# Loading the first half's v in rows of three tokens and ordering it on TensorE with 0/1 matrices, with a new written-out order

## The chip, the cores and the metric

The kernel runs on one core of one Trainium2 chip. A core has TensorE for matrix products (PE in the profile; PEld is its loading of the stationary operand), VectorE (DVE), ScalarE (ACT), GpSimd (POOL) and a queue engine (SP) that issues most of the transfers. Transfers between the main memory and the core's on-chip memory run on 16 DMA engines. TensorE writes only to eight PSUM banks of 128 x 512 float32; the other engines empty them.

The metric is the device time of one execution in microseconds (us), lower is better.

## The reference

Masked attention for 4 batches, 8 heads, 768 tokens and head size 64, and behind it a two-branch feed-forward layer on the joined heads. Three of the heads see all earlier tokens; the other five see the first 4 tokens and a window of 64.

```python
scores = scale * np.matmul(q, k.transpose(0, 1, 3, 2))
...
scores = np.where(mask[None, :, :, :], scores, -1000000000.0)
scores = scores - np.max(scores, axis=-1, keepdims=True)
a = np.exp(scores)
a = a / (np.sum(a, axis=-1, keepdims=True) + 1e-09)
return np.matmul(a, v).astype(np.float32)
...
h1 = x @ w1
h2 = x @ w2
g = np.maximum(h1, h2)
return (g @ w_out).astype(np.float32)
```

Here x has 3072 rows (batch times token) of 512, w1 and w2 are 512 x 1024, w_out is 1024 x 512. All inputs and the output are float32; the kernel computes in bfloat16 with float32 sums.

## The kernel before

The work is cut into eight halves, (batch, half) with 384 tokens each, in the order (0,0), (1,0), (0,1), (1,1), (2,0), (2,1), (3,0), (3,1). A half has three blocks of 128 tokens, and its eight heads are taken as four pairs. The heads are sorted at run time, so that the three full ones come first; the casts read the head number from a register.

For one half the steps are: load q, k and v (`load_half`, L416); cast q and k to bfloat16 into `qb` (`cast_qk`, L632) and v into `vb` (`cast_v`, L646); turn q and k so that the head's 64 values lie on the partitions, for early halves on TensorE (`turn`, L664, and `unturn`, the copy out of PSUM), for the halves in `TURNED_BY_DMA` by a DMA on SP (L687); scores on TensorE (L878, for half (0,0) with the mask added by matmuls at L847); exponentials on ACT (L897); masks on DVE (L916); weighted sums with v on TensorE (L941); division on DVE (L958 and L968) into `x`; turning x on TensorE (L1065) into `xt` or by a DMA (L1084).

The feed-forward layer is rewritten: max(h1, h2) = h2 + relu(x (w1 - w2)). So DVE subtracts the weights once (L1101, four pieces), TensorE multiplies w2 with w_out once (turning w2 at L1118, products at L1145, copied out as `w2o`), and each half then does `up` (L1168: eight groups of four products of 384 columns, relu on ACT or DVE at L1191 and L1193) and `down` (L1223: for each of three blocks twelve products of 512 columns).

The float32 loads go to three slots of one buffer `ld`. Half (0,0) has slot 0, w2 slot 1, w_out slot 0 again piece by piece after the casts of (0,0) have read it, w1 slot 2, half (1,0) slot 0 after the casts of w_out, half (0,1) slot 1 after w2 is used. q and k of early halves come as one transfer each (`whole`, L424): partition p gets the tokens 3p, 3p+1 and 3p+2 of each head, a run of 768 bytes. The tokens are put in order when the turned copy leaves PSUM. v comes in three transfers of 128 tokens (`piece`, L437), a run of 256 bytes for each token and head, since v's tokens must lie on the partitions in order.

The order on every engine is written out. `PLAN` (L172) lists the operations by number, in the order in which they were made, with the engine's letter (p PE, a ACT, v DVE, g POOL, s SP) and for TensorE the PSUM banks; each engine works through its own tokens in that order. A token x stands for a short matmul with no use (L359), which keeps TensorE at work while it waits. Constants such as `DMA_TURN` and the numbers given to `op(...)` are the planner's costs: they made the list, and do nothing on the chip. Numbers 0 and 1 load q and k of half (0,0), 2, 3 and 4 its v; 5 and 10 load the halves of w2; 6, 8, 11 and 13 the quarters of w_out; 15 and 18 the halves of w1; 16, 17 and 19 to 21 are q, k and v of half (1,0); 22 to 26 those of half (0,1). SP issues them in the order 1, 0, 2, 4, 3, 5, 6, 8, 10, 11, 13, 15, 18, 16, 17, 21, 19, 23, 20, 22.

Of the kernel before, what the change touches and what calls it, by code (L numbers as in the profile page):

```python
# [13 lines left out]
ALU = mybir.AluOpType  # L14
# [158 lines left out]
1s x0*3 0s x0*5 2s x0*40 4s 44a 42v 52g x0*2 54a 32v x0 49p0 34a 30g x1*2 50a 59p1 62v x2 39p2 64a x3*2 40a x3  # L173
28v 69p3 60a 29v x4*2 70a x4 27v x4*4 3s 31g 63v x4*2 51a x4*3 33g x4*2 41a x4*5 43a x4*3 61g x4*3 37p4 53g
47p5 5s 67p6 38v x7 57p7 6s x0*3 68v x0 58a x0 71p02 48v 8s x1*2 74p13 73a 72a 10s 35v 65g 56v 77p47 36a 11s
55g 76a 45v 80p65 75a 66v 46v 79a 83p20 13s 81a 90p3 82a 86p17 85a 15s 114v 84a 118v 89p6 87a 115p5 7g 88a
119p0 116v 78a 99p2 100p1 120v 105p 95p 18s 9g 91p 131p7 106v 96v 92v 108v 129p5 94v 130p4 107v 132p 93v 144p0
97v 145p 98v 122v 101p 133p 126v 134p 123p1 102v 16s 12g 103v 127p6 104v 128a 124v x3 111p3 109p2 14g 112v
135p 110v 137p 136p 142p 138p 143v 140p 139a 17s 113v 146p 141a 147p 148a 117v 201p1 203p6 202a 207p3 21s 121v
205p2 208a 204v 212p7 206a 125v 214p5 213a 19s 175g 187a 211p4 159g 151v 161g 215v 218p0 173v 149v 165p1 189v  # L180
179p3 219a 155p6 209p2 180a 156v 23s 188g 166a 160v 150a 193p7 162v 210p5 174a 190v 152a 20s 176v 194v 167p0
157p3 195p6 168a 181p1 158v 216p7 196a 22s 171v 182a 169v 232p03 199v 197v 236p61 183v 234a 185v 217v 238a
x3*2 237a 239p31 233a 244p76 222p 26s 240a 235v 246a 242v 229p 241a 247v 24s 178v 153g 191a 163v 245a 220p
230a 177v 192v 186a 154v 248p03 200a 243v 252p61 198v 250a 256p74 221p 164v 25s 253a 290v 170v 254a 285v 226p
291v 258a 172v 418s 255v 249a 265p3 266p 284a 184v 260p6 261p 267v 257a 251v 294p1 417s 227a 288p4 262v 223p
295a 259v 228s 263v 301g 415s 289a 269v 286g 270p0 268v 272p 300g 271p7 273v 224a 276p 264v 351p51 312g 355p34
277v 293g 275v 353a 358p62 292g 419s 279v 287g 352a 304p1 278v 299g 274v 357a 361p75 311g 354v 280p0 356a 313g
363a 282p4 310v 388p3 281a 303g 389p 283v 231s 314p5 317g 297v 360a 330p4 663s 302v 359a 296v 309g 332p0 298v
307a 319a 322p2 331v 305a 315v 326p6 362a 664s 420g 328p4 426a 442v 421g 316v 443a 324p1 435a 434g 416s 323v
446p7 333a 329v 427g 334p5 225s 325a 306v 447a 318v 430p2 327v 320p0 431a 308v 794s 335v 390p 391p 448v 321a  # L190
432v 364p41 392v 369p76 799s 393v 365a 372p52 394v 346p0 370a 367v 373a 542s 429v 444g 422v 445a 347p 366a
423v 449a 428v 348p 437v 374a 433v 436v 371a 544s 375v 376p43 441g 368v 380p75 378a 384p12 341p6 377a 349v
545s 386a 379v 342p 385a 382a 343p 387v 381a 401p3 667s 383v 344a 403p 395p4 396p 404v 397p 405v 402p0 407p
406v 424p2 408v 398v 336p1 409v 425a 399v 668s 573g 564v 337p 547a 553g 574a 410v 548a 338p 400v 563g 546s
554a 411p5 339v 481p76 543s 485p32 412v 483a 488p04 413p1 486a 438p5 795s 414v 551p6 487a 439v 452p3 489a
460p1 482a 552v 665s 490a 462p2 453v 461a 454p0 440v 463v 666s 549a 550g 491p57 575g 576v 455a 494p64 340s
556g 499p13 493a 566v 502p20 565g 495a 670s 456p7 555v 500a 497v 464p6 496a 484v 671s 503a 450p1 457v 501a
498v 518p4 504a 465v 519p 525p2 492a 451v 798s 672g 526p 673a 520p 505v 506p73 678a 686v 345s 510p06 679v 508a
514p51 687v 527p 507a 521p 466p3 562v 528v 923s 522v 512a 529v 530v 511a 471p7 524v 515a 683s 513v 557p6 516a
509v 567p2 560a 532p0 796s 695a 517v 458p5 568a 523v 350s 577p1 537p 459a 531p4 571v 569v 582g 533p 578a 476p2  # L200
538v 534v 690s 539v 570a 535v 477p 536v 677s 558a 540v 581v 478p 579v 694a 572v 559v 580a 561v 541s 467p 684v
479a 468p 699s 614p51 469v 618p40 621p62 616a 472p 924s 615a 470s 623a 473p 617v 622a 625v 620a 642p3 624v
626p15 619a 474v 630p26 628a 634p04 643p 627a 629v 638p57 635a 644v 647p1 645v 797s 631a 648p 593p0 646v 640a
649v 802s 700v 632a 595p2 650v 651v 594a 585p3 633v 596a 676s 639a 591p7 586v 636a 589p6 641v 637v 597p1 590a
592v 927s 809g 803a 652p0 810v 804g 609p2 475s 598v 587p5 669s 654p 583p3 682s 820a 588v 819a 655v 599p4 656v
584v 691s 653p6 657v 658p 600p 659v 660v 661v 480s 601p 610p 602a 662s 675g 688g 697a 611p 681g 674a 830v 689a
696a 733p71 680a 698s 692v 829a 612v 737p53 740p06 926s 734a 604p4 701v 738a 741a 605p 693a 739a 606p 742a
743p27 735a 607v 746p50 751p36 745a 736v 748a 754p14 808s 716p7 753a 750v 823s 708p0 755a 744a 704p6 752a 709v
814s 710p1 685a 705v 756a 603s 747a 770p2 757v 813s 771p 711a 772p 749v 773p 717a 706p3 774v 775v 758p04 776v
707a 762p65 800s 766p17 760a 712p2 763a 833s 817v 815v 777p3 764a 713v 714p4 759a 765v 778p 767a 779p 761v  # L210
702p6 768a 807s 780v 784p5 715a 782v 783p2 703a 769v 723p0 834s 781v 789p 785p 724p 790v 801s 786v 792v 787v
718p1 824s 788v 791v 719p 870p74 793s 837v 874p63 877p25 835v 871a 720p 875a 876a 872a 725p 921s 812v 832g
721a 873v 728p7 822g 879a 922s 825v 805a 878a 831g 729p 827v 811a 838g 881v 806a 882p63 836a 886p41 890p52
818v 730p 821v 888a 816v 828g 826v 891a 898p1 919s 892a 841p5 880v 883a 726v 884a 843p2 842a 893v 920s 887a
839p6 885v 844a 889v 853p3 840a 925s 845p0 722s 854a 908p5 608s 846a 894p42 903p6 727s 896a 847p3 895a 613s
897v 851p0 848v 928a 929g 855p2 943v 934a 942g 933s 852v 935a 849p4 950a 951v 932s 944g 931v 930a 910p 937a
904p 899p 936v 952a 909p3 911v 850a 945v 914p 865p0 913v 731a 915v 953v 941a 938s 866p 949v 957a 905v 916v
907v 867p 917v 906v 939s 856p 900v 912v 868a 901v 946s 989p47 902v 993p36 947s 991a 996p50 857p 994a 995a
860p1 858v 998a 918s 997a 940v 861p 990a 999p73 992v 1002p60 955s 1000a 1007p25 1004a 1026p4 954s 948v 1027p
1009a 1006v 1028p 732s 862p 1003a 1008a 1005v 1010p70 1001a 1014p56 1033p2 1012a 1029p 1011a 1013v 1034p 1030v  # L220
863a 1035p 859s 1031v 970p3 1016a 1036v 1032v 864s 962p0 1015a 1038v 869s 1037v 968p7 956v 1017v 1018p16 969a
# [22 lines left out]
NQK = 8  # L244
# [1406 lines left out]
```

## Time and profile before

| What | us |
|---|---|
| median of three runs | 182.32 |
| lowest and highest of them | 181.66, 182.47 |
| the profiled execution | 182.37 |
| its span in the profile | 180.6 |
| PE busy in the span | 168.2 |
| ACT busy | 121.4 |
| DVE busy | 118.2 |
| POOL busy | 30.7 |

The profile shows one execution, in microseconds from the start of its span. A group's row has the line of the code, the engine, the operation, what it writes and reads, the shapes, the count, the busy time and the mean duration in ns, and then the idle time of the engine just before these instructions with what ended it. A row of a view by stages has the stage, its length, and for PE, PEld, DVE, ACT and POOL the busy time with the number of instructions; then the granted clock, the share of the DMA engines and the GB/s moved. A row of the timeline has the start, the length, the engine, the operation and the count. A matmul's length includes the time until its result stands in PSUM, so the next one starts before it ends.

### The profile page before, as it was taken

How to read it: one execution, taken by the hardware profiler on the slowest of the kernel's cores; microseconds unless marked ns; L12 is line 12 of the kernel's file. 1: busy time of each engine (PE TensorE's matmuls, PEld its weight loads, DVE VectorE, ACT ScalarE, POOL GpSimd, SP SyncE). 2: the span in 40 equal slices, each digit the busy share in tenths (PEclk: the TensorE clock that was granted, in tenths of full speed). 3: DMA queues.
4: the chain of work that ended last, by engine and by line, in shares of the span. 5: the costliest groups of instructions: out<-in, count | busy, mean ns of one | idle time of the engine just before them, and what ended most of it. 6: DMA issues, size and time to landing. Idle time of an engine off the chain costs nothing.

```text
span 180.6 us, 4847 instructions
## 1 busy us (share of the span) xinstructions
PE 168.2 (93%) x1758; PEld 103.2 (57%) x1778; DVE 118.2 (65%) x339; ACT 121.4 (67%) x267; POOL 30.7 (17%) x74
## 2 busy tenths in 40 slices
PE   7998999989999999999999999999999999999950
PEld 7955564554766566676465445755564566455430
DVE  5336979878998987899497444795567477214220
ACT  3659136699999978899796199929995987212110
POOL 6522240302744103220002020021020000000000
PEclk9999999999999999999999999999999999999995
DMA  4999999999999899998479994449954461331040
GB/s 126 304 302 387 387 385 334 204 318 225 291 314 218 180 331 208 220 256 221 104 191 229 127 239 126 107 100 209 247 184 88 107 222 61 87 119 55 4 174 16
DMA packets 78736, 36.17 MB, mean 200 GB/s; under 512 B 62194, under 2 KB 72690, under 8 KB 78706
## 3 DMA queue, kind: packets, MB, share of 16 engines
q1 hardware_dynamic: 78560, 35.73, 75.9%
q8 instruction: 16, 0.26, 0.7%
q14 instruction: 14, 0.11, 0.3%
q10 hardware_dynamic: 146, 0.07, 0.1%
HBM read 25.17 MB, written 6.29 MB: 174 GB/s over the span
## 4 chain that ended last, share of the span: by engine, by line
PE 58%; DMA 20%; DVE 7%; ACT 5%; issue 3%; POOL 2%; SPq 1%; DVEq 1%; POOLq 0%; ACTq 0%
PE ps L1223 25%; PE ps L1168 19%; DMA ld<-in_q_dram 11%; PE ps L878 6%; PE ps L941 5%; DMA ld<-in_moe_w_out_dram 5%; ACT at L897 4%; DMA qk<-qb 3%; PE ps L664 2%; DVE qb L371 1%; DVE at L916 1%; DVE x L968 1%; SPq L442 1%; PE ps L1065 1%; POOL qb L371 1%
## 5 line engine op out<-in xcount | busy, mean ns | idle before, releaser
L897 ACT ACTIVATE at<-ps 128x512 bf16<-128x512 f32 (+2 forms) x134 | 63.6, 576 | 7.8 <-PE ps L878 7.7
L1168 PE MATMUL ps<-xt,w 128*128 128x384 bf16 x256 | 45.9, 326 | 0.3 <-DVE w L1101 0.2
L1223 PE MATMUL ps<-wob,g 128*128 128x512 bf16 (+2 forms) x195 | 44.7, 370 | 0.5 <-issue 0.3
L916 DVE TENSOR_TENSOR at<-at,tab 128x1024 bf16<-128x1024 bf16 (+5 forms) x49 | 24.0, 508 | 15.0 <-ACT at L897 14.8
L1168 PEld LDWEIGHTS <-w 128*128 128x128 bf16 x256 | 23.8, 98 | 15.9 <-DVE w L1101 0.9
L1223 PEld LDWEIGHTS <-g 128*128 128x128 bf16 x200 | 18.5, 98 | 20.4 <-issue 0.2
L1191 ACT ACTIVATE g<-ps 128x384 bf16<-128x384 f32 x34 | 16.5, 501 | 12.2 <-PE ps L1168 12.1
L1223 PE MATMUL ps<-w2o,xt 128*128 128x512 bf16 (+2 forms) x88 | 23.4, 370 | 0.7 <-issue 0.2
L968 DVE TENSOR_TENSOR x<-ps,rez 128x192 f32 x64 | 22.8, 357 | 1.8
L941 PEld LDWEIGHTS <-at 128*128 128x128 bf16 x477 | 18.1, 97 | 5.5 <-ACT at L897 0.8
L1193 DVE TENSOR_SCALAR g<-ps 128x384 bf16<-128x384 f32 x30 | 16.3, 552 | 7.3 <-PE ps L1168 7.0
L878 PE MATMUL ps<-qk 64*128 64x128 bf16 (+1 forms) x330 | 19.9, 228 | 1.1 <-ACT at L897 0.6
L941 PE MATMUL ps<-vb,at 128*128 128x65 bf16 x387 | 19.9, 193 | 0.4 <-ACT at L897 0.2
L878 PEld LDWEIGHTS <-qk 64*128 64x128 bf16 x330 | 12.5, 94 | 10.7 <-issue 8.6
L371 POOL CAST qb<-ld 128x384 bf16 (+1 forms) x24 | 10.9, 478 | 45.1 <-PE ps L1168 17.8
L369 ACT COPY ot<-ps 128x512 f32<-128x512 f32 (+2 forms) x14 | 7.9, 566 | 14.9 <-PE ps L1223 14.8
L371 DVE COPY ot<-ps 128x512 f32<-128x512 f32 x11 | 7.5, 686 | 13.7 <-PE ps L1223 13.7
L371 POOL CAST vb<-ld 128x192 bf16 x22 | 7.9, 390 | 39.9 <-DMA ld<-in_v_dram 29.2
L369 ACT CAST qb<-ld 128x384 bf16 (+1 forms) x31 | 12.7, 466 | 3.0 <-DMA ld<-in_k_dram 1.9
L1223 PEld LDWEIGHTS <-xt 128*128 128x128 bf16 x100 | 9.0, 98 | 8.7 <-issue 0.2
L369 ACT COPY qk<-ps 128x384 bf16<-128x384 bf16 (+1 forms) x19 | 11.3, 639 | 2.5 <-PE ps L664 2.5
L371 DVE CAST qb<-ld 128x384 bf16 (+1 forms) x25 | 8.4, 369 | 6.1 <-DMA qk<-qb 2.5
(67 smaller groups left out, 156.5 us busy)
## 6 DMA issues: line engine op xcount, KB each, us to landing
ld<-in_v_dram SPq DMA_DIRECT2D x24, 256.0 KB, 6.4
out_dram<-ot SPq DMA_DIRECT2D x23, 256.0 KB, 3.3
ld<-in_moe_w_dram SPq DMA_DIRECT2D x4, 1024.0 KB, 10.6
ld<-in_k_dram SPq DMA_DIRECT2D x5, 768.0 KB, 7.1
ld<-in_q_dram SPq DMA_DIRECT2D x5, 768.0 KB, 7.6
ld<-in_q_dram SPq DMA_DIRECT2D x9, 256.0 KB, 4.8
ld<-in_k_dram SPq DMA_DIRECT2D x9, 256.0 KB, 4.5
ld<-in_moe_w_out_dram SPq DMA_DIRECT2D x4, 512.0 KB, 9.2
```

Source lines behind the costliest of these rows:

```text
L369: nc.scalar.copy(out=out, in_=in_)
L371: eng[e].tensor_copy(out=out, in_=in_)
L664: nc.tensor.transpose(to[:, i], qbs[:, T["qb", n, hf] % NQB, t, i].rearrange("p h d -> p (h d)"), ident)
L878: nc.tensor.matmul(to.rearrange("p (i c) -> p i c", c=128), lhsT=lhsT, rhs=q_of(n, i, m)[rows], start=bk not in under, stop=True, skip_gro ...
L897: nc.scalar.activation(out=at[:, bk, 0:w], in_=bank(("ps", b, hf, t), part=bk)[:, 0:w], func=ACT.Exp, scale=scale,)
L916: eng[e].tensor_tensor(out=at, in0=at, in1=tbl, op=ALU.mult)
L941: nc.tensor.matmul(po[:, hh, i - NT * hf, :], lhsT=ats[:, T["at", b, hf, t] % NAT, bk, e * 128:(e + 1) * 128], rhs=rhs, start=first, stop= ...
L968: nc.vector.tensor_tensor(out=xs[:, HALVES.index((b, hf)) % NX, :, bass.ds(heads[2 * p + hh], 1), :], in0=po[:, hh, :, 0:D].unsqueeze(2), ...
L1168: nc.tensor.matmul(bank(key)[:, 0:HALF], lhsT=w[:, kc, fc * 128:(fc + 1) * 128], rhs=xts[:, HALVES.index((b, hf)) % NXT, :, kc, :], start= ...
L1191: nc.scalar.activation(out=g, in_=ph, func=ACT.Relu)
L1193: nc.vector.tensor_scalar_max(out=g, in0=ph, scalar1=0.0)
L1223: nc.tensor.matmul(bank(key)[:, cols], lhsT=lhsT, rhs=(w2o if kind == "x" else wob)[:, c, cols], start=(e == 0), stop=(e == len(steps) - 1),)
```

## The change

v of half (0,0) comes as q and k do: one transfer with three tokens in a row on each partition (`whole` is called for all three). Eight casts (`cast_rows`) put it into bfloat16 in a third of the `xt` buffer that no half uses yet. Then for each block of 128 tokens three products (`spread_v`) with 0/1 matrices put the tokens in order in a PSUM bank, and one copy (`take_v`) on DVE or ACT brings them to `vb`. The 0/1 matrices are three shifted views of one table of 388 columns, which one memset and one POOL instruction write into a part of the second `g` buffer. The weighted sums of half (0,0) wait for the copies out of PSUM. The first half that writes this `xt` and `g` waits for the products.

Three costs of the planner change, with no instruction of their own: a turn by DMA counts 1.2 instead of 0.55 on SP, and the transfer times of turns are smaller. The whole order is new. In it the numbers from 5 on are smaller by two up to the mask tables; 29 is the table of the 0/1 matrices, 34 to 41 are the casts, 42, 44 and 46 the products, 43, 45 and 47 the copies.

```diff
 PLAN = """
-1s x0*3 0s x0*5 2s x0*40 4s 44a 42v 52g x0*2 54a 32v x0 49p0 34a 30g x1*2 50a 59p1 62v x2 39p2 64a x3*2 40a x3
...
-55g 76a 45v 80p65 75a 66v 46v 79a 83p20 13s 81a 90p3 82a 86p17 85a 15s 114v 84a 118v 89p6 87a 115p5 7g 88a
...
+0s x0*3 1s x0*5 2s x0*40 8s 52a 54v 62g x0*3 32a x0 56p0 60a 25g x1*2 30a 57v x1 68g 64p1 70a x2 48p2 29g 65v
+x3 72p3 49a 73v x4*2 28g x4*6 3s 31a x4 53g x4*4 33a x4 69g x4*3 4s 71a x4*2 55g x4 50p4 63a x5 74p5 61g 51a
+58p6 26g x7*2 66p7 75a 59v x0 76p01 67a 27g 79p23 9s 36a 37v 40g 78a 35v 6s 38a 82p45 34v 81a 39v 85p67 41v
+80a 83a 46p1 86a 16s 127v 44p3 87a 11s 131v 84a 128p2 45a 47v 42p4 77a 129v 132p6 43a 88p75 133v 13s 119v
+91p31 90a 123v 89a 120p0 5v 93a 124p2 92a 121v 105p4 95p6 125a 10g 110p 149p5 111v 136p7 113v 112v 135p1 7a
...
 """
...
-DMA_TURN = 0.25
+DMA_TURN = 0.14
+DMA_TURN_X = 0.165
+TURN_ISSUE = 1.2
+V_ISSUE = 0.8
+SPREAD = ((0, 0),)
...
+    spread = gs[:, NG - 1].rearrange("p c f -> p (c f)")[:, 0:388]
...
+    if SPREAD:
+        nc.vector.memset(spread, 0.0)
...
-            if t < 2 and long:
-                whole(t, (q, k)[t])
+            if t < 2 and long or (b, hf) in SPREAD:
+                whole(t, (q, k, v)[t])
...
+            src = lds[:, slot_of[b, hf], 2, bass.ds(heads[2 * p + hh], 1), :]
+            dst = xts[:, NXT - 1].rearrange("p i k c -> p (i k c)").rearrange("p (j h d) -> p j h d", j=NT, d=D)
+            copy(e, dst[:, :, 2 * p + hh, :], src.rearrange("p o (n d) -> p (o n) d", d=D))
...
+            for j in range(NT):
+                at = 128 * i - j + 2
+                nc.tensor.matmul(
+                    bank(("pv", b, hf, i)), lhsT=spread[:, at:at + 128], rhs=src[:, j], start=(j == 0), stop=(j == NT - 1),
+                )
...
+            copy(
+                e, vbs[:, n:n + HP, :, NT * hf + i, 0:D],
+                bank(("pv", b, hf, i)).rearrange("p (n h d) -> p n h d", h=2, d=D),
+            )
...
+        nc.gpsimd.affine_select(
+            out=spread, in_=spread, pattern=[[1, 388]], compare_op=ALU.not_equal, fill=1.0, base=-2,
+            channel_multiplier=-3,
+        )
...
+            o = pe("TX", mm(*[512] * NT), spread_v(b, hf, i), [*cs, *spread_in], claims=[(key, 1)])
...
-                        {"SP": 0.55}, turn_by_dma(n, hf, t), [*cs, *old_s], data=DMA_TURN * NT,
+                        {"SP": TURN_ISSUE}, turn_by_dma(n, hf, t), [*cs, *old_s], data=DMA_TURN * NT,
```

More of the change, by code (lines that the diff above doesn't have):

```diff
@@ L178 @@
[L178 to L182, printed above, removed]
@@ new lines, in tile_three_full_heads, with spread_half @@
+    if SPREAD:
+        spread_in.append(op({"POOL": 0.9}, spread_table, bias_in, rank=RANK["table"], tag="table", port=("POOL",)))
+    def spread_half(b, hf):
+        got = []
+        old = [o for at in spread_ops.values() for o in at]
+        cs = []
+        for p in range(HP):
+            for hh in range(2):
+                cs.append(op(
+                    dict(CAST_V), cast_rows(b * HP + p, hf, hh), [*loads[b, hf, 2], registers, *old],
+                    tag=f"vcast{b}.{hf}.{p}", rank=rank_of("vcast", b, hf, p), port=("POOL", "DVE"), bias=BIAS if b else None,
+                ))
+        leaves((b, hf), (2,), cs)
+        olds = [o for n in range(b * HP, b * HP + HP) for o in last_w.get(n - NQK, ())]
+        spread_ops[b, hf] = []
+        for i in range(NT):
+            key = ("pv", b, hf, i)
+            o = pe("TX", mm(*[512] * NT), spread_v(b, hf, i), [*cs, *spread_in], claims=[(key, 1)])
+            spread_ops[b, hf].append(o)
+            got.append(op(
+                {"DVE": 0.6, "ACT": act(512)}, take_v(b, hf, i), [o, *olds], frees=[key], tag=f"vtake{b}.{hf}",
+                rank=rank_of("vcast", b, hf),
+            ))
+        return got
```

133 lines of the change are left out of this document (80 added, 53 removed).

## The prediction

> **What bounds the kernel now.** I read the page first, then the stages, then the chain of waits.
>
> ```profile
> span 180.6 us, 4847 instructions
> PE 168.2 (93%) x1758; PEld 103.2 (57%) x1778; DVE 118.2 (65%) x339; ACT 121.4 (67%) x267; POOL 30.7 (17%) x74
> ```
>
> ```profile
> 10.43:28.14 17.71, 16.39 (x187) 9.27 (x187) 12.74 (x31) 8.97 (x18) 4.80 (x6) 1.00 1.06 376
> 28.14:50.10 21.96, 20.35 (x214) 12.53 (x217) 18.98 (x56) 17.97 (x42) 6.04 (x16) 1.00 1.05 272
> 50.10:100.00 49.90, 49.55 (x578) 31.62 (x584) 41.40 (x116) 43.62 (x92) 9.65 (x21) 1.00 0.92 224
> 100.00:120.00 20.00, 19.20 (x214) 11.19 (x215) 11.70 (x32) 14.84 (x34) 1.05 (x3) 1.00 0.79 148
> 120.00:174.00 54.00, 53.35 (x461) 29.78 (x466) 28.10 (x78) 30.65 (x69) 3.00 (x8) 1.00 0.46 124
> ```
>
> ```profile
> 10.26 8.38 DMA ld<-in_moe_w_out_dram
> ...
> 19.77 11.38 DMA ld<-in_q_dram
> 31.14 1.13 DVE w L1101
> ...
> 35.10 8.36 DMA ld<-in_q_dram
> 43.59 0.12 DVE qb L371
> ...
> 50.10 0.63 PE ps L1065 x8
> ```
>
> The stages begin where the first scores start (10.43). PE idles 17.71 - 16.39 = 1.32 us until the first `up` (28.14), 21.96 - 20.35 = 1.61 until 50.1, then 0.35, 0.80 and 0.65. The chain runs through loads and their casts until 50.1 and mostly along PE behind it. So up to 50.1 two limits lie close together: the stream of loads, and PE's own work with 2.9 us of idle time in it. Whoever makes the loads earlier and PE's work longer gains only what the two leave.
>
> **The loads.** v of half (0,0) moves 128 x 8 x 3 runs of 256 bytes, 0.786 MB; after the change 1024 runs of 768, as q and k have.
>
> ```profile
> 5.00:8.00 3.00, 2.85 (x37) 2.57 (x36) 1.30 (x6) 1.96 (x7) 1.37 (x4) 1.00 1.13 320
> 8.00:11.00 3.00, 3.00 (x52) 2.52 (x51) 1.73 (x4) 2.01 (x7) 1.22 (x4) 1.00 1.33 227
> 12.00:27.00 15.00, 14.02 (x167) 8.27 (x162) 10.88 (x28) 6.95 (x14) 4.80 (x6) 1.00 1.05 386
> ```
>
> ```profile
> 1.31 0.56 SPq L429 DMA_DIRECT2D ld<-in_q_dram  x1
> 1.92 6.29 SPq L442 DMA_DIRECT2D ld<-in_v_dram  x3
> 8.25 1.06 SPq L531 DMA_DIRECT2D ld<-in_moe_w_dram  x1
> ...
> 8.54 1.22 POOL L371 CAST qb<-ld 128x192 bf16 x4 [1.63 <-DMA ld<-in_q_dram]
> ...
> 13.32 1.39 DVE L371 CAST vb<-ld 128x192 bf16 x5 [2.17 <-DMA ld<-in_v_dram]
> ```
>
> From 5 to 8 us the stream is mostly q and k (320 GB/s), from 8 to 11 mostly v (227), from 12 on weights (386). 0.786 MB take 3.46 us at 227 and 2.46 at 320: **1.0 us** saved, and w2, w_out, w1 and q, k of (1,0) come that much earlier, since the DMA engines are full (share over 1) and drain SP's transfers roughly in order. The bounds: 0 if the stream doesn't care, and 2.4, if v lands 2.4 us behind the second of q and k (8.5, the POOL row) instead of 4.8 (13.3, the DVE row). SP's three v issues (6.29 us) shrink to one of 0.56, so w2 is issued near 2.5 instead of 8.25; that is worth nothing by itself, as the queue ahead of it is still full then. SP's next wait is w_out, which needs casts of q in slot 0 (around 9) as before; it stands behind both halves of w2 now, whose 2.1 MB cover it.
>
> **The added work.** Nine products of 512 columns, three copies, a memset, a table.
>
> ```profile
> 85.16 3.62 PE L1223 MATMUL ps<-wob,g 128*128 128x512 bf16 x16
> ...
> L371 DVE CAST vb<-ld 128x192 bf16 x11 | 3.1, 345 | 2.2 <-DMA ld<-in_v_dram 2.2
> ...
> L369 ACT CAST w2o<-ps 128x512 bf16<-128x512 f32 x3 | 1.7, 588 | 2.4 <-PE ps L1145 2.4
> L371 DVE CAST w2o<-ps 128x512 bf16<-128x512 f32 x1 | 0.7, 693 | 1.0 <-PE ps L1145 1.0
> L1536 POOL TENSOR_SCALAR_AFFINE_SELECT tab<-tab 128x384 bf16<-128x384 bf16 x2 | 1.0, 520 | 0.1
> L1585 DVE MEMSET tab<- 128x576 uint32 x1 | 0.5, 538 | 1.0 <-PEq L1632 1.0
> ```
>
> - **PE:** sixteen products of this shape take 3.62 us in a row, 0.226 each: nine take **2.0 us**, none of it in waits for the weights' loading.
> - **Casts:** eight before (5 DVE, 2 POOL, 1 ACT), eight after (5, 1, 2), 0.345 each: nothing.
> - **Copies:** two on ACT at 0.588, one on DVE at 0.693. ACT has them among the exponentials of (0,0), where the plan has PE do other work; ACT is busy 8.97 of 17.71 us there, DVE 12.74. Cost nothing while the weighted sums stand behind the turning of w2, as the new list has them; without that cover 1.2 us, two copies in a row on ACT.
> - **Table and memset:** 0.52 us on POOL, and at most 0.54 on DVE (the table has fewer columns than the row's), both before 8 us, where these engines wait for q and k. The mask tables go from DVE to POOL as well; I take nothing, and at worst the scores start by one POOL cast, 0.35 us, later.
>
> Half (0,0)'s `xt` and `g` guests are gone long before the third and second half write there: nothing.
>
> **Where the 2.0 us land.**
>
> ```profile
> 13.52 0.60 PE L847 MATMUL ps<-tab 128*128 128x512 bf16 x2
> ...
> 14.69 0.42 PE L941 MATMUL ps<-vb,at 128*128 128x65 bf16 x8 [0.24 <-ACT at L897]
> ...
> 16.71 1.22 PE L1118 MATMUL ps<-tab,w2b 128*128 128x128 bf16 x16 [0.48 <-DVE w2b L371]
> ...
> 28.14 0.34 PE L1168 MATMUL ps<-xt,w 128*128 128x384 bf16 x1 [0.19 <-DVE w L1101]
> ```
>
> ```profile
> 0.00:10.43 10.43, 8.41 (x88) 7.67 (x88) 0.20 (x1) 1.00 0.89 216
> 10.43:28.14 17.71, 0.67 (x6) 0.21 (x3) 0.00 (x0) 1.00 1.06 376
> 28.14:40.00 11.86, 0.27 (x2) 0.19 (x2) 0.00 (x0) 1.00 1.07 277
> ```
>
> The second view is the useless matmuls alone. There are 88 before the first scores, time that the products can't use, since v has not landed. The new list puts them behind the fourth group of scores, which by the first row here ends near 13.5. From 10.43 to 28.14 PE can give them the 1.32 us of idle time and some 0.2 of three useless matmuls (three weight loads in their row, whose 0.67 counts what hangs over from before 10.43): waits for w2 (0.48), exponentials (0.24) and the subtraction (0.19) are of that kind, and the earlier loads help with the first and last. So PE is 2.0 - 1.5 = **0.5 us** behind at the first `up`'s place at best, with the full 2.0 as the other bound.
>
> From 28 to 50 there are 1.61 us of idle time more, and 0.1 of useless matmuls:
>
> ```profile
> PE ps L359 <- ACT at L897: 0.6, 1, 0.6
> PE ps L1223 <- issue: 0.5, 3, 0.2
> PE ps L941 <- DVE vx L371: 0.4, 1, 0.4
> PE ps L878 <- DVE x L968: 0.3, 1, 0.3
> ```
>
> These are among PE's longest waits from 28 to 174. The one for `vx` hangs on v of (1,0), which follows the weights in the queue; the one at L359 (0.6) lies between the scores of (1,0), where the new list has six useless matmuls instead of two, so a wait stays there. If all went, PE would reach 50.1's place 1.7 - 0.5 = 1.2 us earlier; the loads allow 1.0, and more only with the landing bound. I leave 0.6 us of waits in place: 0.5 + 0.6 - 1.7 = **-0.6 us**.
>
> **The rest of the order** moves the same work. What it can win is the 0.80 + 0.65 us of idle time behind 100; what it can lose has no floor in the profile. The planner's dearer turn is close to the chip:
>
> ```profile
> L687 SPq DMA_TRANSPOSE qk<-qb x24: 1178/1250/2544, 81.4 to 144.7; - x24
> ```
>
> 1.25 us on SP where 0.55 was planned, so the old list was made with a cost less than half of the true one. I take 0, from -1.1 to +0.8.
>
> **The sum:** loads only as a limit, PE +2.0, idle time -2.6 (1.5 + 1.7 - 0.6), order 0: -0.6. The profiled execution took 182.37 us for its span of 180.6, and lies 0.05 from the median of 182.32. 182.37 - 0.6 = **181.8 us**, by itself from 181.2 (no idle time left) to 182.6.
>
> **The rivals.**
>
> - *The later waits go too.* With turns planned at their price the stage from 100 to 120 loses its 0.80, and the last some of its 0.65: 1.1 us more, **180.7**. For it: the turn's row. Against it: 0.5 of the named waits are "issue", which no order takes away.
> - *PE has room that its busy share hides,* so that the products cost nothing. The weight loading is busy for 57% of the span only. Then the loads are the limit, -1.0 or a little more: **181.3**. Against it: sixteen products in 3.62 us leave no gap between them. The Trainium skill, Perfetto Trace Analysis, Identifying the Most-Contended Engine, says that a share of busy matmul time is a bad measure of how near TensorE is to its limit, and that the share of LDWEIGHTS is a better one; by that rule PE at 57% has room. The row at 85.16 doesn't agree for this shape.
> - *The products wait for v (slower).* They stand in PE's fixed order between the fourth and fifth group of scores, so the turning of w2, the last scores and all weighted sums queue behind them. PE gets there near 13.5; the casts take 1.4 (five in a row on DVE). So it decides at a landing of 12.1: earlier costs nothing, later costs one for one. 8.5 + 2.4 gives 10.9; but if v lands at 13.3 as now, PE stands 1.2 us, the stage's idle time is spent there, 0.3 is left to take the products: +2.0 + 1.2 - 1.5 = 1.7, and 0.2 comes back later. **183.9**.
> - *It doesn't do what it says:* the whole v moves no faster. Then PE's 0.5 stays and nothing comes back: **182.9**. Against it: 320 against 227 GB/s.
>
> **How the numbers follow.** About 0.5% (0.9 us: 181.4 and 183.2) is what a measurement of this kernel can tell from no change. Forecast 0.40 (0.08 of it below 181.4, 0.32 within), later waits too 0.22 (faster), room in PE 0.06 (faster), products wait 0.22 (slower), v no faster 0.10 (0.08 within, 0.02 slower, with new waits). Faster 0.36, same 0.40, slower 0.24. The range of 180.5 to 183.9 leaves out half of the waiting case and under half of the best one, 0.2 in all; the forecast's own is 181.2 to 182.6.
>
> **What would show it.** Right: casts of v start near 11 instead of 13.3, GB/s from 8 to 11 near 320, nine products in 2.0 us with less than 0.3 of waiting before them, the first `up` between 26.5 and 29, w1's last subtraction starting before 30.5, and PE busy 2 us more less some useless matmuls. Wrong: an idle PE ahead of the products, scores of (0,0) that start behind 10.8, or an idle time of PE behind 50 that differs from 1.8 by more than 0.5; then the new order, not v, made the time.

## The result and the profile after

| | median us | runs | ratio to before | 95% interval |
|---|---|---|---|---|
| before, first comparison | 182.32 | 5 | | |
| after, first comparison | 180.75 | 5 | 0.9918 | 0.9889 to 0.9947 |
| before, later comparison | 181.63 | 23 | | |
| after, later comparison | 181.38 | 12 | 0.9982 | 0.9951 to 1.0014 |

The first comparison is the one that the prediction was made for: 180.75 us, 0.8% faster, inside the range of 180.5 to 183.9 and 1.05 below the forecast of 181.8. The second, made for the experiments, found 0.2% with an interval that includes no change. In the two profiled executions of after PE's work ends at 172.81 and 172.78 us; in three of before's order (one written with the new source) it ends at 174.13, 173.86 and 173.57, so 0.8 to 1.3 us later. The gain is small, between nothing and 1%.

The profile after, from its page:

```profile
span 179.1 us, 4862 instructions
PE 168.3 (94%) x1759; PEld 103.0 (57%) x1781; DVE 116.9 (65%) x326; ACT 124.5 (70%) x279; POOL 31.5 (18%) x80
```

PE is as busy as before (168.2), although it does nine more products (the two busy sums are taken up again near the end); the span is 1.5 us shorter. The same stages as in the prediction, each from the first scores, the first `up` and so on (columns: stage, its length, then busy time and instructions of PE, PEld, DVE, ACT and POOL, granted clock, DMA share, GB/s):

```profile
9.93:26.56 16.63, 15.46 (x182) 9.08 (x183) 13.21 (x30) 10.81 (x21) 2.87 (x4) 1.00 1.05 384
26.56:48.87 22.31, 21.79 (x218) 13.31 (x219) 19.05 (x53) 17.91 (x44) 4.51 (x12) 1.00 1.07 270
48.87:100.00 51.13, 50.37 (x591) 31.54 (x595) 39.16 (x107) 46.92 (x105) 12.42 (x30) 1.00 0.95 219
100.00:120.00 20.00, 19.61 (x221) 11.53 (x225) 12.65 (x39) 16.19 (x36) 2.26 (x6) 1.00 0.58 137
120.00:172.70 52.70, 52.38 (x457) 29.45 (x459) 27.72 (x74) 27.39 (x60) 1.66 (x4) 1.00 0.50 132
```

Length less busy time is PE's idle time: 1.17, 0.52, 0.76, 0.39 and 0.32 us, 3.16 in all, where before had 1.32, 1.61, 0.35, 0.80 and 0.65, 4.73 in all. The largest drop, 1.1 us, is in the second stage. Some 1.2 to 1.5 us of each total are no waits: the traces lack 20 (before) and 22 (after) records of matmuls, all of 512 columns, and nearly each leaves a gap of about 0.05 or 0.16 us. The stages don't hold the same work in both orders either. And the first scores start 0.50 us earlier (9.93 instead of 10.43), ahead of all these stages. The loads, in the same view of after and then in its timelines of POOL and DVE:

```profile
5.00:8.00 3.00, 2.85 (x43) 2.52 (x42) 1.90 (x6) 1.84 (x6) 2.58 (x7) 1.00 1.10 331
8.00:11.00 3.00, 2.88 (x43) 1.99 (x40) 1.18 (x4) 2.64 (x9) 2.77 (x7) 1.00 1.08 347
```

```profile
8.29 1.22 POOL L378 CAST qb<-ld 128x192 bf16 x4 [0.23 <-DMA ld<-in_k_dram]
...
10.65 1.39 DVE L378 CAST xt<-ld 128x192 bf16 x5 [0.30 <-DMA ld<-in_v_dram]
```

From 8 to 11 us the stream moves 347 GB/s instead of 227, and the casts of v start at 10.65 instead of 13.32. PE's timeline of after around the products:

```profile
12.57 0.40 PE L953 MATMUL ps<-qk 64*128 64x128 bf16 x8
12.90 1.47 PE L717 MATMUL ps<-xt,g 128*128 128x512 bf16 x6
14.21 0.61 PE L1195 MATMUL ps<-tab,w2b 128*128 128x128 bf16 x8
14.66 0.81 PE L717 MATMUL ps<-xt,g 128*128 128x512 bf16 x3
15.30 0.61 PE L1195 MATMUL ps<-tab,w2b 128*128 128x128 bf16 x8
...
18.04 1.22 PE L1195 MATMUL ps<-tab,w2b 128*128 128x128 bf16 x16 [0.49 <-DVE w2b L378]
...
22.44 2.32 PE L1222 MATMUL ps<-wob,w2t 128*128 128x512 bf16 x10
...
26.56 0.81 PE L1245 MATMUL ps<-xt,w 128*128 128x384 bf16 x4
```

No wait stands ahead of the products (a row that had one would show it in brackets). They take the turnings of w2 between them, and the next turnings still wait 0.49 us for w2. The first `up` comes 1.58 us earlier than in before, but that is not the lead of PE: the new order puts ten of the 32 products of w2 and w_out behind it (22 of their weight loads stand ahead of it instead of 32). At 0.216 us each (the row at 22.44 has ten in 2.32 us, the last of them 0.379 long) they are 2.2 us, so with equal work done PE would be at 28.7, 0.6 us behind before.

### The profile page after: what moved, and what is told of

The parts are those of the page before. It is cut to its first block, busy times and chain, and to the rows that moved or that the text cites. A ratio compares the mean times of both kernels' runs of the same rounds, so it can differ in the third digit from the quotient of the medians.

```text
span 179.1 us, 4862 instructions
## 1 busy us (share of the span) xinstructions
PE 168.3 (94%) x1759; PEld 103.0 (57%) x1781; DVE 116.9 (65%) x326; ACT 124.5 (70%) x279; POOL 31.5 (18%) x80
## 4 chain that ended last, share of the span: by engine, by line
PE 59%; DMA 17%; ACT 8%; DVE 5%; issue 4%; POOL 2%; SPq 1%; DVEq 0%; ACTq 0%; POOLq 0%
PE ps L1302 26%; PE ps L1245 18%; DMA ld<-in_moe_w_out_dram 6%; PE ps L953 6%; PE ps L1016 6%; ACT at L972 5%; DMA ld<-in_q_dram 5%; DMA ld<-in_v_dram 4%; PE ps L674 2%; DVE at L991 2%; DMA qk<-qb 1%; ACT qb L376 1%; POOL qb L378 1%; DMA raw<-in_is_retrieval_dram 1%; ACT vx L376 1%
## 5 line engine op out<-in xcount | busy, mean ns | idle before, releaser
L1245 PE MATMUL ps<-xt,w 128*128 128x384 bf16 x256 | 45.2, 326 | 0.0
L991 DVE TENSOR_TENSOR at<-at,tab 128x1024 bf16<-128x1024 bf16 (+5 forms) x49 | 24.3, 509 | 12.9 <-ACT at L972 12.1
L1270 ACT ACTIVATE g<-ps 128x384 bf16<-128x384 f32 x33 | 15.9, 505 | 12.0 <-PE ps L1245 11.9
L378 POOL CAST qb<-ld 128x384 bf16 (+1 forms) x28 | 11.8, 454 | 54.8 <-PE ps L1245 19.6
L376 ACT COPY ot<-ps 128x512 f32<-128x512 f32 (+1 forms) x16 | 9.1, 575 | 16.4 <-PE ps L1302 15.4
L953 PE MATMUL ps<-qk 64*128 64x128 bf16 (+1 forms) x330 | 19.1, 228 | 0.2
L953 PEld LDWEIGHTS <-qk 64*128 64x128 bf16 x330 | 12.1, 94 | 9.3 <-issue 7.0
L376 ACT CAST qb<-ld 128x384 bf16 (+1 forms) x35 | 13.7, 453 | 3.9 <-DMA ld<-in_q_dram 2.5
L378 DVE COPY qk<-ps 128x384 bf16<-128x384 bf16 (+1 forms) x14 | 9.6, 697 | 4.2 <-PE ps L674 4.0
L378 POOL CAST vb<-ld 128x192 bf16 x18 | 5.8, 357 | 32.3 <-DMA ld<-in_v_dram 29.1
L378 DVE COPY ot<-ps 128x512 f32<-128x512 f32 (+1 forms) x9 | 6.1, 674 | 8.0 <-PE ps L1302 8.0
L1033 DVE RECIPROCAL rez<-ps 128x6 f32<-128x6 f32 x32 | 5.7, 187 | 6.3 <-ACT at L972 4.0
## 6 DMA issues: line engine op xcount, KB each, us to landing
ld<-in_moe_w_dram SPq DMA_DIRECT2D x4, 1024.0 KB, 12.1
```

The source lines that it names most:

```text
L376: nc.scalar.copy(out=out, in_=in_)
L378: eng[e].tensor_copy(out=out, in_=in_)
L953: nc.tensor.matmul(to.rearrange("p (i c) -> p i c", c=128), lhsT=lhsT, rhs=q_of(n, i, m)[rows], start=bk not in under, stop=True, skip_gro ...
L991: eng[e].tensor_tensor(out=at, in0=at, in1=tbl, op=ALU.mult)
L1033: nc.vector.reciprocal(out=z, in_=po[:, :, :, D])
L1245: nc.tensor.matmul(bank(key)[:, 0:HALF], lhsT=w[:, kc, fc * 128:(fc + 1) * 128], rhs=xts[:, HALVES.index((b, hf)) % NXT, :, kc, :], start= ...
```

## The experiments

Each ratio is against runs of before on the same chip.

### The change taken apart: order, load and products

Four kernels cross the order, the load and the products. `WHOLE_V` is a constant that loads v of half (0,0) in one transfer without the products; the two kernels that have this leave v's tokens out of order, so they show times only. In the new order without products, the eight casts stand where the row casts stood. Here and below only the part of `PLAN` that matters is shown, without regard to its line breaks.

New order, v in pieces, no products:

```diff
-SPREAD = ((0, 0),)
+SPREAD = ()
+WHOLE_V = ()
 PLAN = """
-0s x0*3 1s x0*5 2s x0*40 8s 52a
+0s x0*3 1s x0*5 2s 4s 3s x0*40 10s 41a
...
-83a 46p1 86a 16s 127v 44p3 87a 11s 131v 84a 128p2 45a 47v 42p4 77a 129v 132p6
+81a 18s 122v 82a 13s 126v 79a 123p2 72a 124v 127p6
```

> New order, but v of half (0,0) in three pieces as before, cast straight to its place, no products. Theory A (two limits up to 50 us, loads and PE, and the rest of the order worth about -0.7 us): PE has 2.0 us less to do but w2 comes 1 us later, so 181.2 to 182.0 us. Theory B (the order alone makes the gain; load and products cancel): 180.7 us or less, since the 2.0 us of products are saved. Theory C (the earlier loads alone make the gain, products are free): 182.3 us or more.

New order, v as a whole, no products:

```diff
-SPREAD = ((0, 0),)
+SPREAD = ()
+WHOLE_V = ((0, 0),)
 PLAN = """
-83a 46p1 86a 16s 127v 44p3 87a 11s 131v 84a 128p2 45a 47v 42p4 77a 129v 132p6
+79a 16s 120v 80a 11s 124v 77a 121p2 70a 122v 125p6
```

> New order, v of half (0,0) in one transfer of 768-byte rows, but cast straight to its place and without products: the tokens of this half's v stay out of order (this part of the reference is not computed). Against the changed kernel's 180.75 it shows what the products cost at the end. Theory A: the loads become the limit, so only a part of the 2.0 us comes back: 179.8 to 180.4 us. If PE alone is the limit: 178.8 us. Theory C (products free): 180.7 us.

Old order, v as a whole, no products (against before):

```diff
+WHOLE_V = ((0, 0),)
 PLAN = """
-1s x0*3 0s x0*5 2s x0*40 4s 44a
+1s x0*3 0s x0*5 2s x0*40 42a
...
-28v 69p3 60a 29v x4*2 70a x4 27v x4*4 3s 31g
+67p3 58a 27v x4*2 68a x4 25v x4*4 29g
```

> Old order, v of half (0,0) in one transfer of 768-byte rows, cast straight to its place, no products: the tokens of this half's v stay out of order (not computed as the reference has it). It shows what the earlier loads alone bring. Theory A: 1.0 us of the 3.2 us of idle time up to 50 us goes, 181.1 to 181.6 us. Theory B (the order alone): 182.3 us. Theory C: 180.8 us or less.

Old order with the load and the products (against before):

```diff
+SPREAD = ((0, 0),)
 PLAN = """
-80p65 75a 66v 46v 79a 83p20 13s 81a 90p3 82a
+85p65 80a 41v 37v 46p2 44p0 42p3 84a 47v 88p17 11s 86a 45a 87a 43a 91p26
```

> Old order with the whole of the change to v in it: one transfer, table, row casts, products behind the fourth group of scores, copies, and the first weighted sums behind the first turning of w2. Theory A: products +2.0 us on PE, idle time -1.5, the loads' gain partly used: 182.0 to 182.8 us. Theory C: 180.8 us. If the products wait for v or the weighted sums for the copies: 183.5 us or more.

The four were measured on one chip. After was not measured with them, so its place in the table is less sure than theirs:

| | v in pieces | whole, no products | whole with products |
|---|---|---|---|
| old order | 1 (before) | 180.26 us: 0.9897 [0.9831, 0.9962] | 182.88 us: 1.0052 [1.0019, 1.0086] |
| new order | 183.83 us: 1.0086 [1.0045, 1.0127] | 181.67 us: 0.9994 [0.9959, 1.0028] | after: 0.9918 and 0.9982 |

Along each row, the whole load is worth about 1%. Down the first two columns, the new order alone costs about 1%. The products cost 1.5% (2.6 us) in the old order. In the new one no cost can be measured between runs on different chips; in the profiles the kernel without them ends PE's work at 172.28 us and after at 172.81, so some 0.5 us is left. So the gain comes from the load. The new order alone takes about as much away, and its waits take up most of the products.

The expectations were set against the first comparison's 182.32 and 180.75. The kernel with the new order and v in pieces came out at theory C's 182.3 or more, the second above all of its theories, the third at theory C's 180.8 or less, the fourth just above theory A's 182.0 to 182.8. So no theory holds in all four: the order alone is no gain (against B), the products are not free in the old order (against C), and A did not have the new order alone dearer than the old.

Why the products are nearly free in the new order is seen on PE from 12.5 to 18.5 us, first in the new order without products and then in after:

```profile
12.50:18.50 6.00, 3.72 (x53) 2.24 (x52) 3.81 (x6) 4.64 (x10) 0.00 (x0) 1.00 1.05 386
```

```profile
12.50:18.50 6.00, 5.51 (x62) 3.12 (x61) 4.40 (x7) 5.41 (x12) 0.00 (x0) 1.00 1.05 387
```

The nine products (53 and 62 instructions) fill 1.79 of 2.28 us of idle time. The timeline of the kernel without them shows what PE waits for there, and that nothing behind it comes earlier:

```profile
14.03 1.22 PE L1195 MATMUL ps<-tab,w2b 128*128 128x128 bf16 x16 [1.13 <-DVE w2b L378]
...
18.03 1.22 PE L1195 MATMUL ps<-tab,w2b 128*128 128x128 bf16 x16 [1.15 <-DVE w2b L378]
...
26.56 0.81 PE L1245 MATMUL ps<-xt,w 128*128 128x384 bf16 x4
```

The turnings at 18.03 and the first `up` at 26.56 stand where after has them (18.04, 26.56). The new order lets PE wait for w2 early, and the products are put into that wait.

In the old order the list is short of such waits. The rows are the first `up` of the whole load without products, and then with them (there L1244 is the same line):

```profile
27.16 4.07 PE L1245 MATMUL ps<-xt,w 128*128 128x384 bf16 x24 [0.19 <-DVE w L1178]
```

```profile
13.42 2.12 PE L716 MATMUL ps<-xt,g 128*128 128x512 bf16 x9
...
24.48 0.62 PE L1194 MATMUL ps<-tab,w2b 128*128 128x128 bf16 x8 [0.82 <-DVE w2b L377]
...
29.85 2.45 PE L1244 MATMUL ps<-xt,w 128*128 128x384 bf16 x14 [0.19 <-DVE w L1177]
```

The load alone brings the first `up` 0.98 us forward (28.14 to 27.16; four other executions that start as before does had it at 28.11, 27.93, 27.78 and 28.90, so a part of this may be the execution). The products take 2.12 us, a new wait of 0.82 us for w2's casts on DVE comes on top, and the first `up` is 2.69 us later than without them.

That wait is not simply a lack of room. The two casts of w2 ahead of it took 1.07 and 1.52 us in this execution; the same casts take 0.68 to 0.70 us in the other thirteen profiles. They ran beside two casts of w_out on POOL (21.39 to 22.43 and 22.73 to 23.88 us), for 0.78 and 0.97 us. In the other profiles they overlap a cast on POOL by 0.37 us at most. That the overlap slowed them is likely but was not tested. Without the wait the products would cost about their own 2 us there (2.69 - 0.82 = 1.9, an estimate).

### The products done twice

```diff
-            for j in range(NT):
+            for j in (*range(NT), *range(NT)):
```

> The changed kernel with each of the nine products done twice, so that the second set overwrites the first: 18 products, 4.0 us of PE instead of 2.0, same output, same order of everything else. Theory A (products cost nothing while they fill PE's wait for w2): without them PE waited 1.32 and 1.33 us for w2, 2.65 in all; one set fills 2.0 of it and 0.49 of the wait was left ahead of the turnings at 18.04, so a second set of 2.0 us fills that and pushes the turnings by 1.5 us; the first product of w1 with the turned w2 comes 1.5 us later than the changed kernel's, and the end by 1.0 to 1.5 us: 181.8 to 182.3 where the changed kernel takes 180.75. Theory C (products are free wherever they stand, PE has room): the turnings still start near 18.0 to 18.5 and the time stays within 0.3 us. Theory D (each product costs its full time on the path, and the new order only made room elsewhere): 2.0 us later, 182.75.

182.42 us, ratio 1.0035 [1.0001, 1.0069], against 181.38 us for after on the same chip: 1.04 us more for 2.0 us of PE, with some 0.8 us to either side by the two intervals. In its profile the wait of 0.49 us for w2 is gone, as expected:

```profile
19.94 1.12 PE L1194 MATMUL ps<-tab,w2b 128*128 128x128 bf16 x16
20.89 0.78 PE L1015 MATMUL ps<-vb,at 128*128 128x65 bf16 x20
22.70 1.24 PE L1221 MATMUL ps<-wob,w2t 128*128 128x512 bf16 x5 [1.03 <-DVE rez L1032]
```

The turnings start 1.9 us later than at 18.04; 0.5 of that is this execution's first scores, which started at 10.45 instead of 9.93. PE's work ends at 174.69, 1.88 us later than in after, with the same 0.5 in it. So the room that the new order has for products is filled by one set, and a second set goes into the end. The wait that follows grew as well, from 0.34 to 1.03 us, since the division's first step comes later. (PE's own waits without products were 1.13 and 1.15 us, not the 1.32 and 1.33 of the expectation.) Theory A's 1.0 to 1.5 us fits the medians and the profile. Theory C's room is not there: the turnings start near 19.9 and not near 18. Theory D's full 2.0 isn't reached in the medians, but lies near the edge of what they allow.

### The two orders joined near 50 us

The changed kernel up to the last `up` of the first stage and the order of before behind it, and the reverse; the banks behind the join are dealt out again:

```diff
 PLAN = """
-329p5 547s 448v 431v 366p26 447v 330a 369p47 374p31 368a 550s 297v
+358a 297g 292g 304g 362a 366p57 359v 361a 318g 368a 393p2 308g 394p 322g
```

> The changed kernel's load, products and order up to the last of the first piece's products of w1 near 50 us, and from there the order of before; same output. In the changed kernel PE is 0.44 us ahead of before at 51 us, 0.65 at 53 to 63 and 1.1 to 1.3 at the end. Theory F (the gain is made by 60 us, and the rest keeps it): ends 0.5 to 0.7 us ahead of before, ratio 0.996 to 0.997. Theory G (half of the gain is made behind 50 us by the new order there: the stall of before at 107 to 109 us is gone): with the old order there the stall comes back, the end is 0 to 0.5 ahead, ratio 0.997 to 1.000, and the kernel that has the old order first and the new behind is 0.6 to 0.8 ahead. Theory H (the stall of before at 107 to 109 was one transfer's bad luck, and goes by itself once all is earlier): ends 1.1 to 1.3 ahead like the changed kernel, ratio 0.993.

```diff
 PLAN = """
-432v 364p41 392v 369p76 799s 393v 365a 372p52 394v 346p0 370a 367v 373a 542s
+370a 430p4 663s 366a 447v 337p 425a 338p 368v 307g 371a 448v 362a 339a 431v 390p 391p 372p65
```

> The first load in three pieces, no products and the order of before up to the last of the first piece's products of w1 near 50 us, and from there the changed kernel's order; same output. PE should stand where it stands in before up to 50 us. Theory F (the gain is all made by 60 us): ends like before, ratio 1.000 within 0.003. Theory G (half of it is made by the new order behind 50 us): ends 0.6 to 0.8 us ahead of before, ratio 0.996 to 0.997, with no wait of PE near 107 to 109 us. Theory H (the order behind 50 us does nothing, early arrival does): like before, with waits near 107 to 109 us as before has them (0.42 and 0.17).

Both failed as experiments: 188.99 us, 1.0405 [1.0365, 1.0445], and 187.38 us, 1.0262 [1.021, 1.0314]. The timeline of POOL shows why for the first:

```profile
55.33 1.52 POOL L377 CAST vb<-ld 128x192 bf16 x5 [7.90 <-issue]
```

One order's loads of v stand late on SP, and the other order's weighted sums come early on PE, so at the join PE stood 4.98 us for a cast of v. In the second kernel PE stood 3.91 us for a relu on ACT, which itself waited 4.2 us for a load of v (this profile is of its longest execution, 189.38 us). They say nothing of where the gain is made, so that question went to the table above and to the two controls at the end.

### After once more

The changed kernel, with no edit.

> The changed kernel once more, on the chip that runs the three beside it, so that they are set against it and not against its runs on another chip. The same by every theory: 0.9918 of before, from 0.989 to 0.995; if it comes out near 1.000 like the kernel with the new order and no products did (0.9994, on one chip), then that difference lay in the chip and not in the products.

0.9982 [0.9951, 1.0014], as in the first table. Its profile has the stalls of the first one (0.52 ahead of the turnings at 18.02, first `up` at 26.54). That is near the ratio of the new order without products (0.9994 [0.9959, 1.0028]), so the difference between 0.9918 and 0.9994 needn't come from the products; two comparisons of after itself differ by nearly as much.

### PE kept at work during the long wait

In the new order with v in pieces PE stood 3.84 us for w2. Here 60 dummy products stand in that place:

```diff
-78a 81a 18s 122v 82a 13s 126v 79a 123p2 72a 124v 127p6
+78a 81a 18s 122v 82a 13s 126v 79a x2*60 123p2 72a 124v 127p6
```

> The kernel with the new order, v in pieces and no products (183.83, ratio 1.0086), with 60 dummy products of 128 columns on PE, about 3.3 us, put where PE stood 4.03 us for w2 at 12.74. w2 comes no earlier, so nothing of the dummies lengthens the wait's end. Theory K (behind a wait of 4 us the granted clock falls to half for about 5 us, and that, not the wait, is the second half of the loss): the clock stays at full speed from 16.8 to 22 us, PE's work of those 5 us takes about 2.5 us less, and the time comes out at 181.3 to 182.0. Theory L (the low clock has another cause, such as the transfers or the weights of the turnings): the clock falls all the same, and the time stays near 183.8. A middle result, 182.5 to 183, would say that the work behind is held by w2's loads in any case and half of the lower clock is hidden in waits.

The stages of the kernel without the dummies, and then with them:

```profile
12.70:16.80 4.10, 0.26 (x8) 0.09 (x5) 1.31 (x5) 3.66 (x8) 0.00 (x0) 0.78 1.05 387
16.80:21.00 4.20, 4.20 (x30) 2.33 (x32) 3.44 (x6) 0.88 (x2) 0.00 (x0) 0.50 1.05 386
```

```profile
18.00:22.00 4.00, 4.00 (x67) 2.66 (x65) 3.69 (x6) 2.66 (x5) 0.03 (x1) 1.00 1.07 392
```

The granted clock (the column behind POOL's) stays at 1.00 with the dummies and is 0.50 without: theory K's mechanism is shown. Its price isn't: 183.67 us, 1.0087 [1.0059, 1.0115], against 1.0086 without. This execution was late by itself: its first scores started 0.54 us later (10.45 instead of 9.91), and w2's first cast 0.47 us later (16.52 instead of 16.05). The turnings followed the dummies at 17.48, some 0.3 us after the end of that cast, PE then waited 0.74 us for a cast of w_out, and the first `up` came only 0.5 us earlier (29.14 instead of 29.63). A clock that stays up, in the place where it was down, didn't move the medians. That the late loads are what the pieces lose in the new order is the better account, but it is argued and not shown.

### The stall of before near 108 us

In before PE stands at 107 to 109 us for exponentials; the old order with the whole load and the old order with products don't have it. A load of v is put behind two turns that follow it on SP:

```diff
-584v 691s 653p6 657v
+584v 691s 669s 653p6 657v
...
-592v 927s 809g 803a 652p0 810v 804g 609p2 475s 598v 587p5 669s 654p
+592v 927s 809g 803a 652p0 810v 804g 609p2 475s 598v 587p5 654p
```

> The kernel before, with one load of v on SP's queue (issued at 97.53) put behind the two turns that follow it (issued at 98.01 and 99.56). Same output. In before the first of these turns took 6.26 us to land, and PE stood 0.42 and 0.17 us for scores at 108 to 109, with the next turn's copies waiting as well. Theory M (the load ahead of the turn is what holds the turn): the turn lands in about 3 us, the waits of PE near 107 to 109 go, and the end comes 0.6 to 0.8 us earlier, ratio 0.996. Theory N (the turn was late because of all that was on the queue there, and any shift of a microsecond undoes it, as in the old order with the whole load, which had no such wait): the waits change size or place in no fixed way, and the time is within 0.3% of before.

183.41 us, 1.0059 [1.0023, 1.0095]: 0.6% slower, where theory M had 0.996 and theory N no more than 0.3% either way. The stall is gone, yet this execution's first `up` already came 0.77 us later than in before, and its 128th product of w1 (99.18 us in before) 1.55 us later, with nothing swapped so far. The products in the old order, 1.35 us late at that point, have lost the stall too, so the swap isn't told from the shift. Two controls followed. Before, with no edit:

> The kernel before, unchanged, with a profile of its own. It tells what of the first comparison was the change and what was that one execution. In the profiled execution of before PE lost 1.1 us more at 107 to 109 us than three other kernels with the same order there (1.12 against the old order with the whole load, 1.12 against the old order with the products, 1.03 against the swap). Theory N (that wait belongs to one execution): it is absent or of another size here, w1's first product starts within 1 us of 28.14, and the end is 0.5 to 1.2 us earlier or later than in the first profile for that reason alone. Theory P (the wait belongs to the order of before, at its own time): PE stands 0.4 to 0.6 us twice at 107 to 109 again, and the change's gain behind 100 us stands.

And its order written with the changed kernel's source (the fresh planner costs do nothing on the chip):

```diff
-DMA_TURN = 0.25
+DMA_TURN = 0.14
+SPREAD = ()
+WHOLE_V = ()
```

> The order of before and its loads in pieces, written with the changed kernel's source (its tables and tiles, none of its new work in use): a control for the experiments that were written that way, the swap of the load of v above all, which was 0.6% slower though its first 97 us are before's. If the source changes nothing: 1.000 within 0.003 of before, and the swap's loss is the swap's. If it comes out near 1.006, the swap cost nothing and the place of the tiles or the program's length did.

Before came out at 182.0 us, 1.0018 [0.9982, 1.0054], and its order from the new source at 181.94 us, 1.0015 [0.9977, 1.0053]: the source changes nothing. PE's and DVE's waits from 104 to 112 us, of before in its first profile and then in the second (columns: who waits for what, us in total, times, longest):

```profile
DVE qb L371 <- DMA qk<-qb: 2.5, 1, 2.5
...
PE ps L878 <- ACT at L897: 0.6, 2, 0.4
```

```profile
DVE qb L371 <- DMA qk<-qb: 2.6, 1, 2.6
...
PE ps L878 <- ACT at L897: 0.4, 2, 0.3
```

The stall comes back, with the same turn by DMA landing late, though smaller than theory P had it (0.4 us in all, where it said 0.4 to 0.6 twice). It belongs to the old order at its own pace, not to one execution; the two executions of before lie within 0.12 us of each other up to that 128th product. It shrinks as PE gets there earlier: in the order from the new source, 0.24 us ahead of before at that product, one wait of 0.2 us is left, and in the whole load in the old order, 0.82 us ahead, none. Why the swap is 0.6% slower stays open.

## Why the prediction came out as it did

- **The loads, 1.0 us earlier: right, a little low.** 347 GB/s where 320 was taken, the casts of v near 11 as named, and in the old order the first `up` 0.98 us earlier with nothing else changed. The bound of 2.4 was for v's own landing; v's casts did come 2.67 us earlier, but in the old order w2's casts gained 1.4 (15.96 to 14.59) and the first `up` 1.0.
- **The nine products, 2.0 us: right,** 2.12 us in a row in the old order, and no wait ahead of them in either. The rival *the products wait for v* needed a landing of v behind 12.1; its casts started at 10.65.
- **0.5 us behind at the first `up` at best, 2.0 at worst: right in size, not in where the room came from.** With equal work done after is 0.6 us behind, as worked out above, and the old order with the products is 1.71 behind (29.85 instead of 28.14). But the prediction took 1.5 us from the idle time and the dummies where before has them. PE's idle time from the first scores to the first `up` fell only from 1.32 to 1.17. The new order moves the turnings of w2 ahead and so makes a wait of 2.28 us that before didn't have, the products fill 1.79 of it, and the scores start 0.5 us earlier. The step read the new list's places for the products and the old list's waits, so that its number came out is luck in part.
- **28 to 50 us, 1.1 us of idle time gone: right in size, wrong in cause.** Idle time fell from 1.61 to 0.52. (Of both, 0.26 us are gaps of three missing records.) The prediction put it down to loads that come earlier. With the whole load in the old order that stage still idles:

```profile
27.16:49.00 21.84, 20.52 (x219) 12.86 (x223) 19.25 (x56) 17.96 (x43) 6.14 (x16) 1.00 1.05 267
```

  1.32 us, and the new order without products 0.34. So it is the order that closes these waits.
- **The rest of the order, 0: mis-sized, and one of its terms was no wait.** Behind 50 us PE's idle time is 1.47 instead of 1.80, within the 0.5 that the prediction allowed. The stage from 100 to 120 fell from 0.80 to 0.39, while 48.87 to 100 rose from 0.35 to 0.76. The last stage fell from 0.65 to 0.32, but 0.57 of the 0.65 and nearly all of the 0.32 are gaps at missing records. In the trace of the swap above, which has before's order there and lacks no record, PE idles 0.07 us from 120 us on. So the 0.65 that the prediction counted as a thing to win was hardly there, and the waits named "issue" are such gaps too. The rival *the later waits go too* is nearest in time (180.7). Its cause, turns planned at their price, isn't shown: the old order loses the wait at 108 too once it comes 0.8 us earlier or 1.35 later.
- **PE busy 2 us more: wrong.** It is busy 0.1 us more. The dummies fell by 0.8 us (9.4 to 8.6, 93 to 87 of them), though in the second execution of after only to 9.2. The sum of a group tells less than it seems to. The groups of before, and then of after (busy time behind the bar):

```profile
L1168 PE MATMUL ps<-xt,w 128*128 128x384 bf16 x256 | 45.9, 326 | 0.3 <-DVE w L1101 0.2
...
L878 PE MATMUL ps<-qk 64*128 64x128 bf16 (+1 forms) x330 | 19.9, 228 | 1.1 <-ACT at L897 0.6 <-DVE x L968 0.3
```

```profile
L1245 PE MATMUL ps<-xt,w 128*128 128x384 bf16 x256 | 45.2, 326 | 0.0
...
L953 PE MATMUL ps<-qk 64*128 64x128 bf16 (+1 forms) x330 | 19.1, 228 | 0.2
```

  256 and 330 products, at the same mean length, cover 0.7 and 0.8 us less. For the 256 products of w1 that is no gain: they stand in 27 stretches before and in 22 after, and the last product of a stretch reaches 0.16 us over the start of the next group (0.326 long, 0.163 from start to start). Counted from each start to the next they take 42.2 and 42.3 us. Counted in this way the scores do take 1.3 us less (14.9 to 13.7), the turnings of q and k 0.8 less, and products of w2o 1.0 more. The new order without products has the scores at 13.7 too, and the old order with the whole load at 14.6, so most of it goes with the order. A wait shorter than a product's own length counts as busy in these sums, so some of it may be short waits that the order removes; what it is stays open. Some 0.45 us is doubtful, as after's trace lacks two matmul records more than before's (nine more products and six fewer dummies make three more, the page counts one).

Together, over the whole span: PE's work ends 1.3 us earlier (172.8 instead of 174.1), busy time +0.1 and so idle time -1.4, where the forecast had idle time -2.6 and busy time +2.0. Idle time fell by 1.2 less and busy time rose by 1.9 less than forecast: two misses of opposite sign that partly cancel, so that the total came near is luck in part. The 0.7 between -0.6 and -1.3 is what they leave. About 0.5 of the 1.3 lies ahead of the first scores, which no term of the sum has: they start at 9.86 to 9.93 in five of the seven executions of the new order and at 10.45 in two, and at 10.1 to 10.7 in the old. The whole distance to the median, 1.05, is no larger than that between the two comparisons of after (0.64%, 1.2 us). *PE has hidden room* came out in effect and not in cause: the products were nearly free where PE had a wait, visible in the timeline, and dear where it had none. The Trainium skill's rule on the share of weight loading (Perfetto Trace Analysis, Identifying the Most-Contended Engine) doesn't decide this: that share is 57% in after as in before, while a second set of products cost 1.04 us.

No run beat after with the same work. The shortest, 180.26 us, is the load in the old order without the products: what that order would take if v were put in order at no cost.

## What to carry to other kernels

Added work on the busiest engine is free only inside a wait that can be pointed at; look for it in the new order, not in the old one, and test it by doing the work twice. A faster load is worth what the first consumer in a fixed order can use: cross the load and the order before crediting either, since here each alone gave -1% and +1%. When the order changes, read a lead at equal work: the first `up` alone showed one of 1.6 us that was not there. When a stall vanishes with a change, see whether any shift of a microsecond makes it vanish before a cause is named.

## What the runs showed of the hardware that wasn't expected

A long wait of TensorE is followed by a slow clock. In the kernels with waits of 3.84, 4.98 and 3.91 us the granted clock was 0.50 for 6.83 us each time. It fell 2.04, 3.29 and 2.80 us after PE had stopped, while PE still waited, and rose 5.0 to 5.7 us after it had gone on. Around the two waits of 1.13 and 1.15 us it stayed at 1.00. What the slow clock costs at the end was not shown. The clock's line on three pages, of the pieces in the new order, of the first joined kernel and of the pieces with dummies (40 slices, tenths of full speed):

```profile
PEclk9996699999999999999999999999999999999995
```

```profile
PEclk9999999999975999999999999999999999999996
```

```profile
PEclk9999999999999999999999999999999999999996
```

Sixty dummies in the wait kept it up. The Trainium skill, TensorE: Matmul & The Clock Gate, Part 1 on the HAM clock gate, puts the idle window at about 3.4 us and the gated clock at half. The half agrees; as the shortest wait that lowers the clock 3.4 us doesn't hold here, since the first of the three fell after 2.04 us.

Two casts of w2 on DVE were longer beside casts of w_out on POOL: 1.07 and 1.52 us where they overlapped for 0.78 and 0.97 us, against 0.68 to 0.70 us in all other profiles. This was seen in one execution, and nothing was done to test it.
